# Other random offsets in the order of work: sliding-window attention with an MLP-mixer on one Trainium2 core

## The chip, the cores and the metric

The kernel runs on one core of one Trainium2 chip. The metric is the device time of one execution in microseconds (us). Lower is better. The core has five engines that run side by side: TensorE (PE, matrix products), VectorE (DVE), ScalarE (ACT), GpSimd (POOL) and SyncE (SP). In this kernel the last two do hardly more than issue transfers.

## What is computed

The inputs are q, k and v of 8 batches x 8 heads x 576 positions x 64. The attention is causal with a window of 128 positions and a linear penalty for distance (ALiBi). A mixer of two stages follows: one product pair along the positions, one along the channels, each with its residual.

```python
scores = scale * np.matmul(q, k.transpose(0, 1, 3, 2))
bias = slopes[:, None, None] * (-np.abs(rel))[None, :, :]
mask = (rel >= 0) & (rel < 128)
scores = np.where(mask, scores + bias[None], -1e9)
attn = softmax(scores)                              # per head
x = np.matmul(attn, v) -> (8, 576, 512)             # heads side by side
h = np.maximum(x.T @ w_tok1, 0.0) @ w_tok2          # 576 -> 256 -> 576
u = x + h.T
h2 = np.maximum(u @ w_ch1, 0.0) @ w_ch2             # 512 -> 1536 -> 512
return u + h2
```

## The kernel before

**Tiles.** The 576 positions of a batch are four blocks of 128 and a rest of 64. The rests of two batches share one block, the tail. Matmul operands are bf16, sums are in PSUM (eight banks, the tiles named `ps`).

**Attention of a block.** q and k are turned so that the 64 channels of a head lie on the partitions. In the first blocks PE does it (L632, and L638 copies the result to `qkT`); later SP issues a transposing DMA (L621). PE multiplies the scores (L672), ACT takes the exponential (L695, into `pe`), DVE multiplies with the mask (L705), PE multiplies with the values and a column of ones (L739), and DVE takes the reciprocal of the sum (L752) and scales (L755, into `xb`; ACT can do that in its place, L761).

**Token mixing of a batch.** The first product is L784, with L794 for the tail's rows (`xt`, copied in L779). ACT (L802) or DVE (L803) applies the relu. The second product is L827 (L823 for the tail). DVE adds the residual (L845, into `ub`). For the two opening batches the result is turned by PE (L862, copied by L868), and there L830 adds the residual on PE and ACT copies (L842). From batch 2 on SP issues transposing DMAs (L853): four of `uT` per batch, and in every second batch one of the tail, `uTt`.

**Channel mixing of a batch.** The first product is twelve chunks of four matmuls of 128x512 (L1024; in the very first batch L1009 for two of them), each followed by a relu on ACT (L1030) or DVE (L1031). For the last batch the first product goes in another form, by sums of halves (L910) and products L946, evicted in L961 to L990. The tail's first product is L1067, its relu L1072. The second product is seven smaller ones by sums of halves, which DVE makes (L1049 of the hidden values, L570 and L588 of the weights): L1212, evicted with the residual added by DVE in L1180 and stored from L1192. The tail's own is L1112 and L1119, stored from L1129. The last batch ends with L1241, L1245 and L1248.

**Where the order comes from.** Nothing of this is issued where it is written. Every operation is entered in a list with its engine, a cost, its inputs and a rank, which says when it is due (class `Plan`, L66 to 314). `run` (L118 to 299) plays the engines forward with the written costs: an engine takes, of the operations that could start first, the one of the lowest rank. Some operations have a second engine (`other`) and go to the one that would be done earlier. POOL keeps the fixed order of `LOADS` (L364) and of the later loads; SP's order follows from the ranks. `emit` (L301) writes the instructions out in planned order; on the chip each engine then runs its own list in that order and waits for what it needs. `emit` also fills planned gaps of PE up to plan time 60 us with dummy matmuls on a tile of zeros (`spin`, L1292 and L1296).

**Rounds and offsets.** `side` makes a batch's attention and token mixing, `main` its channel mixing. The opening is `side(0)`; then a round for each batch b holds `main(b)` and `side(b + 1)` (L1269 to 1283), so the next batch's attention is woven into this batch's products. The opening is part 0, the round of batch b is part b + 1. Each part has a seed:

```python
        dice = [random.Random(x) for x in SEEDS]
        for o in ops:
            if SEEDS[o.part]:
                o.rank += dice[o.part].uniform(-SHIFT, SHIFT)
```

The rank of every operation of the part is moved by a random amount of up to 1500 either way (`SHIFT`; ranks count in ns of PE's work). A seed of 0 leaves the ranks of its part alone. Ranks of the opening lie a million lower than all others.

**At the end** (L1285 to 1290), two operations on ACT of nine tiny copies each and two on DVE of five tiny memsets each are entered with a rank behind all others and may start at 262 and 266.5 us of plan time. They write to the tile of zeros and are read by nothing; ACT issues the last store (L1248) after them.

Of the kernel before, what the change touches and what calls it, by code (L numbers as in the profile page):

```python
# [10 lines left out]
ACT = mybir.ActivationFunctionType  # L11
# [54 lines left out]
class Plan:  # L66
# [6 lines left out]
    def buf(self, name, choice=None):  # L73
        return Buf(self.rings[name], choice or self.rings[name].each)
# [43 lines left out]
    def run(self):  # L118
        ops = self.ops
# [4 lines that stand above are left out]
# [210 lines left out]
RANKH = 0  # L334
RELU = 350
SUMS_AT = 60e3
SEEDS = [45795, 495947, 190309, 331881, 0, 67117, 67408, 179769, 445757]
SHIFT = 1500.0
UNIT_LATE = False
SECOND_LATE = True  # L340
# [28 lines left out]
def kernel(  # L369
# [76 lines left out]
    zero = const.tile([P, P], BF16, name="zero")  # L446
# [25 lines left out]
    pe_, act_, dve_ = nc.tensor, nc.scalar, nc.vector  # L472
# [53 lines left out]
    for i_, name in enumerate("qk"):  # L526
# [3 lines left out]
            out=buf()[:, i, :, :], in_=raw.rearrange("p (h d) -> p h d", h=H)), -100 + i_, makes=buf, after=4.8e3 + 600 * i_)  # L530
# [64 lines left out]
    for e in range(2):  # L595
        def go(e=e):
            for i in range(2):
                dve_.tensor_copy(out=maskt[:, e, :, 0, i * R : (i + 1) * R], in_=masks[:, e, :, 0, 0:R])
            dve_.tensor_copy(out=maskt[:, e, :, 1, :], in_=masks[:, e, :, 1, :])
            dve_.memset(maskt[0:R, e, :, 1, R:P], 0.0)  # L600
# [682 lines left out]
        base += n  # L1283

    for eng, n, cost, at, go in (  # L1285
            ("ACT", 9, 200, 262e3, lambda: act_.copy(out=zero[:, 0:1], in_=zero[:, 2:3])),
            ("ACT", 9, 200, 262e3, lambda: act_.copy(out=zero[:, 0:1], in_=zero[:, 2:3])),
            ("DVE", 5, 60, 266.5e3, lambda: dve_.memset(zero[:, 1:2], 0.0)),
            ("DVE", 5, 60, 266.5e3, lambda: dve_.memset(zero[:, 1:2], 0.0))):
        plan.op(eng, n * cost, lambda n=n, go=go: [go() for _ in range(n)], 1e9, after=at)  # L1290
# [41 lines left out]
```

## Time and profile before

| | before |
|---|---|
| time, median of 3 runs | 278.81 us (278.72 to 279.33) |
| time of the profiled execution | 278.47 us |
| span in its trace | 276.7 us |
| of the span: PE, DVE, ACT, POOL busy | 97%, 76%, 50%, 42% |
| PE clock granted | 1.00 |
| channel products L1024 on PE | 77.4 us in 306 recorded matmuls |
| masks L705 of 128x1024 on DVE | 30.8 us in 46, 683 ns each |
| transposing DMAs L853, issue to landing | 2.3 / 3.5 / 6.3 us (least, median, most) |

The page counts busy time for each engine. The chain is the work that ended last, followed back from the last instruction; what stands there on PE is time that only less work on PE can save, and what stands there on another engine or a transfer is time in which PE had to wait or was not yet started. "ps<-uT,WC" means that PSUM was written from the tiles `uT` and `WC`. In a timeline row the columns are the start, the length, engine and line, the operation, and how many instructions are put together in the row; square brackets hold the idle time before it and what ended it. SPq is SP issuing a transfer.

### The profile page before, as it was taken

To read this page: it belongs to the slowest core of one execution; us is meant where nothing else is said; L and a number is where in the kernel's file an instruction comes from. 1 tells how busy PE (TensorE), PEld (TensorE's weight loads), DVE (VectorE), ACT (ScalarE), POOL (GpSimd) and SP (SyncE) were. 2 spreads that over 40 slices of the span, in tenths; PEclk is the share of its full clock that TensorE was granted. 3 is DMA by queue.
4 is the path that set the end of the run, shared out by engine and by line. 5 is a ranking of instruction groups with operands and counts; after the bars stand their busy time and mean duration, and the time that the engine had idled before them with its cause. 6 is when DMAs were issued, how large, how long until landed. Compare 5 with 4: busy or idle time off the path is not lost.

```text
span 276.7 us, 6959 instructions
## 1 busy us (share of the span) xinstructions
PE 268.5 (97%) x2789; PEld 179.6 (65%) x2825; DVE 209.0 (76%) x496; ACT 139.2 (50%) x237; POOL 115.8 (42%) x146
## 2 busy tenths in 40 slices
PE   7999999999999999999999999999999999999994
PEld 3665655775686555585567655576667645679884
DVE  7577689978897469853989478763989549886984
ACT  5572884436950298107951096206860079205660
POOL 8998965940356037900585009600472220013000
PEclk9999999999999999999999999999999999999999
DMA  9999999999899999999999979999499750043014
GB/s 132 159 141 164 182 192 189 155 124 207 138 110 111 181 243 133 124 142 181 173 136 151 206 193 100 138 144 243 65 117 97 194 147 2 2 114 135 1 50 143
DMA packets 167553, 38.45 MB, mean 139 GB/s; under 512 B 155808, under 2 KB 166688, under 8 KB 167520
## 3 DMA queue, kind: packets, MB, share of 16 engines
q0 software_dynamic: 116112, 20.03, 94.9%
q1 hardware_dynamic: 50224, 17.57, 33.6%
q10 hardware_dynamic: 1184, 0.39, 0.6%
q8 instruction: 22, 0.36, 0.6%
q14 instruction: 11, 0.09, 0.1%
HBM read 35.85 MB, written 9.44 MB: 164 GB/s over the span
## 4 chain that ended last, share of the span: by engine, by line
PE 89%; DMA 4%; DVE 2%; POOL 1%; ACT 1%; issue 1%; POOLq 0%; ACTq 0%
PE ps L1212 26%; PE ps L1024 22%; PE ps L739 6%; PE ps L672 6%; PE ps L784 5%; PE ps L827 5%; PE ps L1067 4%; PE ps L1112 4%; PE ps L946 3%; DMA WC<-in_moe_w_ch_dram 3%; PE ps L1296 2%; DMA qk<-in_q_dram 2%; PE ps L632 1%; PE ps L794 1%; POOL qk L515 1%
## 5 line engine op out<-in xcount | busy, mean ns | idle before, releaser
L1024 PE MATMUL ps<-uT,WC 128*128 128x512 bf16 x306 | 77.4, 379 | 1.3 <-DMA WC<-in_moe_w_ch_dram 0.3
L695 ACT ACTIVATE pe<-ps 128x1024 bf16<-128x1024 f32 (+1 forms) x76 | 63.4, 888 | 29.9 <-PE ps L672 29.6
L515 POOL DMA_DIRECT2D v<-in_v_dram x40 | 34.1, 866 | 93.6 <-PE ps L739 88.5
L1030 ACT ACTIVATE r<-ps 128x512 bf16<-128x512 f32 x75 | 44.4, 601 | 41.1 <-PE ps L1024 39.1
L1024 PEld LDWEIGHTS <-WC 128*128 128x128 bf16 x328 | 29.1, 98 | 30.6 <-issue 1.4
L705 DVE TENSOR_TENSOR pe<-pe,mask 128x1024 bf16<-128x1024 bf16 (+1 forms) x64 | 38.2, 609 | 8.8 <-ACT pe L695 8.3
L1212 PEld LDWEIGHTS <-r 128*128 128x128 bf16 x372 | 35.9, 98 | 7.2 <-issue 0.2
L515 POOL DMA_DIRECT2D qk<-in_k_dram x39 | 34.5, 891 | 3.0 <-DMA v<-in_v_dram 1.7
L515 POOL DMA_DIRECT2D qk<-in_q_dram x39 | 34.0, 878 | 0.7 <-DMA WC<-in_moe_w_ch_dram 0.6
L1212 PEld LDWEIGHTS <-s 128*128 128x128 bf16 x288 | 27.5, 98 | 6.0 <-issue 1.3
L755 DVE TENSOR_TENSOR xb<-ps,rt 128x256 bf16<-128x256 f32 (+1 forms) x72 | 29.1, 417 | 0.7
L739 PEld LDWEIGHTS <-pe 128*128 128x128 bf16 (+1 forms) x560 | 22.3, 98 | 9.0 <-DVE pe L705 2.6
L739 PE MATMUL ps<-v,pe 128*128 128x65 bf16 (+1 forms) x560 | 26.3, 194 | 0.4 <-DVE pe L705 0.2
L1212 PE MATMUL ps<-WC,r 128*128 128x256 bf16 x192 | 25.4, 273 | 0.0
L1212 PE MATMUL ps<-WT,s 128*128 128x256 bf16 x192 | 24.6, 273 | 0.1
L845 DVE TENSOR_TENSOR ub<-ps,xb 128x512 bf16<-128x512 f32 x34 | 21.2, 683 | 1.8 <-PE ps L827 1.8
L1212 PE MATMUL ps<-WT,r 128*128 128x256 bf16 x180 | 22.4, 273 | 0.0
L672 PEld LDWEIGHTS <-qkT 64*128 64x128 bf16 x560 | 14.8, 94 | 11.2 <-issue 9.8
L1180 DVE TENSOR_TENSOR ob<-ps,ub 128x512 f32<-128x512 f32 x21 | 14.3, 686 | 9.4 <-PE ps L1212 9.2
L672 PE MATMUL ps<-qkT 64*128 64x128 bf16 (+1 forms) x304 | 19.4, 216 | 0.4
L1072 ACT ACTIVATE r2t<-ps 128x512 bf16<-128x512 f32 x12 | 7.2, 603 | 22.7 <-PE ps L1067 22.7
L752 DVE RECIPROCAL rt<-ps 128x4 f32<-128x4 f32 (+1 forms) x76 | 12.5, 175 | 7.6 <-PE ps L739 7.0
(102 smaller groups left out, 347.8 us busy)
## 6 DMA issues: line engine op xcount, KB each, us to landing
v<-in_v_dram POOLq DMA_DIRECT2D x32, 128.0 KB, 5.0
out_dram<-ob SPq DMA_DIRECT2D x16, 256.0 KB, 2.6
qk<-in_k_dram POOLq DMA_DIRECT2D x31, 128.0 KB, 5.1
qk<-in_q_dram POOLq DMA_DIRECT2D x31, 128.0 KB, 5.0
WC<-in_moe_w_ch_dram POOLq DMA_DIRECT2D x8, 384.0 KB, 8.8
out_dram<-raw SPq DMA_DIRECT2D x7, 256.0 KB, 2.7
out_dram<-ob POOLq DMA_DIRECT2D x5, 256.0 KB, 3.6
out_dram<-raw POOLq DMA_DIRECT2D x3, 256.0 KB, 2.9
```

Source lines behind the costliest of these rows:

```text
L515: nc.gpsimd.dma_start(out=to()[p0 : p0 + n, :, :], in_=rows(src, b, s0, n))
L672: pe_.matmul(wide(e)[:, i, kind, a:z], lhsT=ts[kb]()[e * D : (e + 1) * D, NHP + i, :], rhs=ts[blk]()[e * D : (e + 1) * D, i, a:z], start=n ...
L695: act_.activation(out=pb()[:, e, :, lo:, c0:c1_], in_=wide(e)[:, :, lo:, c0:c1_], func=ACT.Exp, scale=scale)
L705: dve_.tensor_tensor(out=o, in0=o, in1=heads(mk, es), op=ALU.mult)
L739: pe_.matmul(view()[a:z, at, i, :], lhsT=pb()[:, e, i, kind, a:z], rhs=vb()[:, h, 0 : D + 1], start=m == 0, stop=m == len(mms) - 1, skip_g ...
L755: dve_.tensor_tensor(out=x4(), in0=view()[r0:r1_, :, :, 0:D], in1=rt()[r0:r1_, 0:n, :, :].broadcast_to([r1_ - r0, n, 4, D]), op=ALU.mult)
L784: pe_.matmul(t1[j]()[:, :], lhsT=W1[:, c, j * P : (j + 1) * P], rhs=xb()[:, blk, :], start=c == 0, stop=False)
L845: plan.op("DVE", 690, lambda blk=blk, ht=ht, hs=hs: dve_.tensor_tensor(out=ub()[:, blk, :], in0=ht()[:, hs], in1=xb()[:, blk, :], op=ALU.a ...
L1024: pe_.matmul(ct()[:, :], lhsT=WC1[:, cb, t * P : (t + 1) * P], rhs=uT()[:, cb, :], start=cb == 0, stop=cb == NCB - 1)
L1030: plan.op("ACT", 600, lambda t=t, ct=ct: act_.activation(out=r2()[:, t, :], in_=ct()[:, :], func=ACT.Relu), rk, part=(r2, t), uses=[ct], o ...
L1180: dve_.tensor_tensor(out=v, in0=both(bk), in1=src, op=ALU.add)
L1212: pe_.matmul(of(bk, c), lhsT=l(t, c), rhs=w(t), start=first, stop=g == 1 and t == HK - 1, skip_group_check=True)
```

## The change

```diff
-SEEDS = [45795, 495947, 190309, 331881, 0, 67117, 67408, 179769, 445757]
+SEEDS = [751877, 741206, 821723, 331881, 0, 148233, 244960, 0, 319733]
...
-            ("ACT", 9, 200, 262e3, lambda: act_.copy(out=zero[:, 0:1], in_=zero[:, 2:3])),
-            ("ACT", 9, 200, 262e3, lambda: act_.copy(out=zero[:, 0:1], in_=zero[:, 2:3])),
+            ("ACT", 11, 200, 262e3, lambda: act_.copy(out=zero[:, 0:1], in_=zero[:, 2:3])),
+            ("ACT", 10, 200, 262e3, lambda: act_.copy(out=zero[:, 0:1], in_=zero[:, 2:3])),
```

The seeds of the opening, of the rounds of batches 0 and 1 and of batches 4 to 7 are others; the round of batch 6 has none now. Those of batches 2 and 3 stay. Three more tiny copies stand at the end of ACT's list. No operation is added to or taken from the computation, and `LOADS` stays as it is. What differs is the order in which operations stand on PE, DVE, ACT and SP, which engine takes those that have two, and where the dummy matmuls lie.

## The prediction

> **What bounds the kernel now.** First the page: engines, then the chain of work that ended last.
>
> ```profile
> span 276.7 us, 6959 instructions
> PE 268.5 (97%) x2789; PEld 179.6 (65%) x2825; DVE 209.0 (76%) x496; ACT 139.2 (50%) x237; POOL 115.8 (42%) x146
> ...
> PE 89%; DMA 4%; DVE 2%; POOL 1%; ACT 1%; issue 1%; POOLq 0%; ACTq 0%
> ```
>
> PE is busy 97% of the span and is 89% of the chain. A new order takes no matmul away, so it can gain only where PE waits, and lose only where it adds a wait. The view of waits on PE names the largest of them (total us, times, longest):
>
> ```profile
> PE ps L1296 <- DVE zero L479: 1.0, 1, 1.0
> ...
> PE ps L1024 <- DMA WC<-in_moe_w_ch_dram: 0.3, 1, 0.3
> ...
> PE ps L739 <- DVE pe L705: 0.2, 1, 0.2
> ```
>
> The first is the start, before any seed matters. The rest are tenths. How much the touched stretches hold in all, the view by windows tells: in each row the second number is the window's length, then PE's busy time.
>
> ```profile
> 20.00:30.00 10.00, 9.89 (x111) 6.06 (x113) 6.09 (x16) 4.85 (x10) 8.95 (x11) 1.00 1.93 169
> 30.00:40.00 10.00, 9.47 (x133) 6.05 (x132) 8.52 (x28) 8.43 (x14) 7.41 (x11) 1.00 1.78 184
> 40.00:60.00 20.00, 19.48 (x195) 13.37 (x197) 18.37 (x41) 9.30 (x15) 13.66 (x18) 1.00 2.01 169
> 60.00:80.00 20.00, 19.79 (x238) 12.96 (x240) 18.04 (x48) 14.53 (x22) 6.13 (x7) 1.00 1.46 154
> ...
> 160.00:180.00 20.00, 19.75 (x192) 11.04 (x194) 15.70 (x38) 11.79 (x17) 11.49 (x14) 1.00 1.55 140
> 180.00:200.00 20.00, 19.84 (x214) 13.93 (x216) 13.00 (x29) 10.80 (x17) 2.81 (x4) 1.00 0.88 153
> 200.00:220.00 20.00, 19.84 (x214) 14.25 (x212) 15.63 (x34) 5.86 (x8) 8.62 (x11) 1.00 1.29 128
> 220.00:240.00 20.00, 19.69 (x194) 10.85 (x197) 15.31 (x37) 13.06 (x23) 1.82 (x3) 1.00 0.27 66
> 240.00:260.00 20.00, 20.00 (x200) 16.91 (x198) 15.47 (x29) 7.78 (x15) 2.87 (x4) 1.00 0.29 87
> ```
>
> A quiet window (180 to 220) shows 0.16 us idle in 20. Above that are idle: 0.03 in 20 to 30, 0.45 in 30 to 40, 0.36 in 40 to 60, 0.05 in 60 to 80, 0.09 in 160 to 180, 0.15 in 220 to 240, nothing elsewhere. That is 1.13 us, 0.4% of the time: **the most that this change can gain**. The loss has no such bound.
>
> **The change part by part.** Built, the changed kernel has 2824 matmuls for 2825. The multiset of real matmuls, and the number of switches between their shapes, are the same. PE's list is the same up to 20.2 us, in nine blocks from 34.6 to 44.8 us, and from 90.1 to 161.0 us (batches 2 and 3), and again in the last products. POOL's list is the same. So PE's own work changes by one dummy matmul only: 592 columns in two become 408 in one, 184 less. At 0.65 / 1536 us a column (three matmuls of 512 columns from 44.80 to 45.45, rows below) that is -0.08 us.
>
> **Opening, up to 36 us.** The chain and PE's timeline:
>
> ```profile
> 25.92 0.89 POOL v L515
> ...
> 28.52 7.42 DMA WC<-in_moe_w_ch_dram
> ```
>
> ```profile
> 35.99 1.04 PE L1024 MATMUL ps<-uT,WC 128*128 128x512 bf16 x4 [0.32 <-DMA WC<-in_moe_w_ch_dram]
> ...
> 41.18 0.66 PE L739 MATMUL ps<-v,pe 128*128 128x65 bf16 x16 [0.24 <-DVE pe L705]
> ...
> 44.54 0.42 PE L739 MATMUL ps<-v,pe 128*128 128x65 bf16 x8
> 44.80 0.81 PE L784 MATMUL ps<-xb,W 128*128 128x512 bf16 x3
> 45.45 0.41 PE L739 MATMUL ps<-v,pe 128*128 128x65 bf16 x8
> ```
>
> PE arrives at the fifth kind of chunk 0.32 us before the weights' load (issued 28.52, landing 35.94). The load keeps its place on POOL, three loads behind the one of 25.92. The chain has L862 ahead of that one, but L862 does not read the `v` tile that it fills; the products that do (L739) end before 20.2 us in either order, and what it waits for is an earlier load. So nothing that moves sets the load's time. Whatever the new order saves before 36 us, the 0.08 included, ends in this wait: **0**. It costs something only if PE comes over 0.32 us later than now.
>
> **36 to 45 us.** PE's blocks are the same; on DVE one weight sum (L570) changes places with one sum of hidden values (L1049), both about 0.55 us. The waits at 41.18 and 44.54 stay: 0. At 44.80 the old order has three L784 (0.65) between two groups of values; the new one has one (0.22). The second group needs the second of these masks:
>
> ```profile
> 43.80 1.28 DVE L705 TENSOR_TENSOR pe<-pe,mask 128x1024 bf16<-128x1024 bf16 x2
> ```
>
> It ends at 45.08, and the 44.50 to 44.54 step that the chain shows as "issue" takes 0.05 after a mask. The new order reaches the values at 44.80 + 0.22 = 45.02 and waits until 45.13: **+0.11**. From either side: 0 (DVE earlier by its last operation's overlap) to +0.2.
>
> **45 to 90 us.** DVE is busy 18.37 and 18.04 of 20 us here, so this is where orders differ. Some alternatives change engines:
>
> ```profile
> L755 DVE TENSOR_TENSOR xb<-ps,rt 128x256 bf16<-128x256 f32 (+1 forms) x72 | 29.1, 417 | 0.7
> ...
> L845 DVE TENSOR_TENSOR ub<-ps,xb 128x512 bf16<-128x512 f32 x34 | 21.2, 683 | 1.8 <-PE ps L827 1.8
> ```
>
> DVE gets one copy L638 and one relu L803 more (each one operation of 512 or 1024 columns, about 0.68 by the nearest row), one L755 more (0.42), and gives three L868 (0.42 each, as many columns out of PSUM as an L755 costs) and one L1031 (0.68) to ACT: 1.78 less 1.94, nothing. Following each product back to its DVE and ACT inputs, with the durations of this execution, I find places with 30 to 70 ns to spare and none plainly late. I take **+0.1**, between 0 and one displaced operation (0.4).
>
> **94 us.** The four turned blocks of batch 2 are issued with one store among them, but their sums come earlier: 0 to +0.2, taken as **+0.05**.
>
> **Batch 5, 174 to 190 us.** PE, SP and DVE, and the line of the transposes (least, median, most):
>
> ```profile
> 174.63 1.89 PE L827 MATMUL ps<-r,W 128*128 128x512 bf16 x8
> 176.45 0.62 PE L823 MATMUL ps<-r,W2t 128*64 128x512 bf16 x4
> 177.01 1.04 PE L1024 MATMUL ps<-uT,WC 128*128 128x512 bf16 x4
> ...
> 183.78 1.47 PE L1212 MATMUL ps<-WT,r 128*128 128x256 bf16 x12
> 185.09 1.89 PE L1024 MATMUL ps<-uT,WC 128*128 128x512 bf16 x7
> ...
> 190.28 1.07 PE L1067 MATMUL ps<-uTt,WC 128*128 128x128 bf16 x16
> ```
>
> ```profile
> 175.98 2.52 SPq L853 DMA_TRANSPOSE uT<-ub  x2
> 178.60 1.22 SPq L853 DMA_TRANSPOSE uTt<-ub  x1
> 179.87 3.54 SPq L853 DMA_TRANSPOSE uT<-ub  x2
> ```
>
> ```profile
> L853 SPq DMA_TRANSPOSE uT<-ub x24: 1190/1232/2225, 87.2 to 247.8; - x24
> ...
> DMA to landing us min/median/max: 2.3/3.5/6.3
> ```
>
> Between L827, whose sums are turned, and L1024, which uses them, lie 10.46 us. The new order moves the four L1024 of 177.01 (0.87) and twelve L1212 (12 of 0.109, 1.31) ahead of L827, and sixteen L1067 (1.07 less the 0.16 by which a row is longer than its steps, 0.91) in between. So L827 starts at 176.81, L1024 can start at 186.00, and 9.19 us are left. The first transpose then is issued at 176.81 + 1.35 = 178.16, and the fifth four steps later: of 1.29 each (175.98 to 179.87 is three), at 183.32. In the old order the last was issued at 179.87 + 3.54 - 1.26 = 182.15, and L1024 came at 185.09, straight after twelve steps of L1212: so it took at most 2.9, and by the row at least 2.3. Then it lands between 185.6 and 186.2: 0 to +0.2, and I take **0**. `uTt`, third in line, is now needed at 185.09: issued at 180.74, it lands at 184.2 by the median.
>
> The row of landings runs from 2.3 to 6.3. The Trainium skill, "DMA: Bandwidth & Descriptors", section "Issuing engines are not separate DMA queues", says that transfers started by SP and POOL run on the same 16 DMA engines and interleave. By that rule the transposes share with POOL's loads wherever they are issued, and at 6.3 the last would land at 189.6, for +3.6; the bound of 2.9 above speaks against that for the last of them.
>
> **Batch 6, 220 us.**
>
> ```profile
> 220.45 0.59 PE L1112 MATMUL ps<-WC,r2t 128*128 128x512 bf16 x2
> 221.03 1.02 PE L1024 MATMUL ps<-uT,WC 128*128 128x512 bf16 x4
> ```
>
> Two steps of 0.217 end at 220.88; 0.15 is a wait for the turned blocks. The new order leaves some 2.6 us more between their sums and this L1024, so it goes: **-0.15**. The 0.09 over the quiet level in 160 to 180 I count by half, **-0.05**.
>
> **The end.**
>
> ```profile
> 264.18 2.00 ACT L1286 COPY zero<-zero 128x1 bf16<-128x1 bf16 x9
> ...
> 273.64 0.36 ACTq L1248 DMA_DIRECT2D out_dram<-ob  x1
> ```
>
> Three more copies of 0.22 us end near 268.9; ACT's store waits for DVE until 273.64. Cover 4.7 us: **0**. The last batch's products are mixed anew; window 240 to 260 shows no idle time, and I find no input late: 0.
>
> **Sum**: 0 + 0.11 + 0.1 + 0.05 + 0 - 0.15 - 0.05 = +0.06 us on the profiled execution's 278.47 (span 276.7 and 1.77 outside it, unchanged). That execution lies 0.34 under the median of 278.81, so the forecast is **278.9 us**.
>
> **Rivals.** (1) *Slower: the turned blocks of batch 5 come late.* One of the five issues took 2.2 us instead of 1.23 (the row's most; it is in the 3.54). If it does again, the last is issued at 184.3 and lands at 186.6 to 187.2, a wait of 0.6 to 1.2 where none was: about 279.7. It decides as soon as issue and landing together pass 186.0 - 178.16 = 7.8 us; they would take 7.5 to 8.1 without the long issue. For it: the distance shrinks by 1.27 us; against: the long issue is one of 24. (2) *Slower: DVE becomes late in 45 to 90 us.* Two inputs, each late by one operation of 0.42 that is now ahead of it, less 0.07 to spare, give +0.7: about 279.6. It decides where more than 0.07 us of DVE's work is put ahead of an input that PE takes next. For it: DVE's 90%; against: its total does not grow. (3) *Faster: the waits go.* If the new order clears the excess of 40 to 60 (0.36), 160 to 180 and 220 to 240 (0.24), it gives -0.6 on 278.81: 278.2. Against: the two mask waits stand in blocks that do not change. (4) *Faster: the weights' load was not the limit.* If it lands earlier, as DVE leaves POOL other times to issue, up to 0.32: 278.3 with the 0.15 of batch 6. (5) *The change does nothing*, the orders being equal: excluded, they differ in four stretches.
>
> **How the numbers follow.** Forecast 0.47; (1) 0.18; (2) 0.14; (3) 0.17; (4) 0.04. About 0.2%, 0.56 us, is what a measurement of this kernel tells from no change. Faster: (3), 0.17; within: the forecast and (4), 0.51; slower: (1) and (2), 0.32. The range runs from (3) to just above (1): 278.2 to 279.8; beyond lie the 1.13 bound below and a late `uTt` above. The likeliest case alone: 278.5 to 279.3.
>
> **What would show it.** In the changed kernel's trace: L1024 still waiting for the load that lands near 35.9; a new wait of about 0.1 at the values near 45.0; windows 40 to 60 and 60 to 80 within 0.2 of 19.48 and 19.79; L1024 after sixteen L1067 near 186.0 with no idle time before it (a transpose named there makes (1) right); no wait near 221. The prediction is wrong if a new wait of over 0.5 us stands anywhere, or if the load near 36 us lands at another time.

## The result, and the profile after

The changed kernel takes **281.84 us** (median of 6 runs, 281.26 to 282.92), the kernel before **279.19 us** beside it (6 runs, 278.72 to 280.33). The ratio is 1.0096, with an interval of 1.0072 to 1.0119: **2.65 us slower**, between 2.0 and 3.3. The prediction, 278.9 in a range of 278.2 to 279.8, was wrong. The profiled execution took 281.66 us.

The page of the profile after: span, busy time by engine, and the chain of work that ended last.

```profile
span 279.9 us, 6968 instructions
PE 268.7 (96%) x2790; PEld 179.8 (64%) x2824; DVE 210.7 (75%) x496; ACT 138.7 (50%) x237; POOL 115.8 (41%) x146
...
PE 72%; DVE 8%; POOL 7%; DMA 5%; issue 3%; SPq 2%; ACT 1%; DVEq 0%; ACTq 0%; POOLq 0%
```

PE is busy 268.7 us for 268.5, so its own work is as forecast; the span grew by 3.2 us of waiting. PE's share of the chain fell from 89% to 72%. Outside the span lie 1.76 us for 1.77. The view of waits on PE, after:

```profile
PE ps L632 <- DMA qk<-in_q_dram: 1.5, 2, 1.1
...
PE ps L1212 <- DVE raw L1180: 0.7, 1, 0.7
PE ps L1024 <- DMA uT<-ub: 0.3, 1, 0.3
```

The first two were not in the forecast, and for the third it had 0.05. The windows, after (length, then PE's busy time):

```profile
20.00:30.00 10.00, 8.76 (x102) 5.39 (x99) 5.79 (x15) 3.92 (x9) 8.07 (x11) 1.00 1.84 160
30.00:40.00 10.00, 9.50 (x134) 6.19 (x135) 8.24 (x26) 7.41 (x13) 8.17 (x10) 1.00 1.79 184
40.00:60.00 20.00, 19.41 (x176) 12.30 (x179) 19.71 (x44) 10.35 (x16) 13.70 (x17) 1.00 1.93 160
60.00:80.00 20.00, 19.75 (x250) 13.19 (x251) 16.82 (x45) 13.82 (x23) 5.03 (x6) 1.00 1.37 148
80.00:100.00 20.00, 19.35 (x172) 13.16 (x174) 13.53 (x28) 5.68 (x13) 6.36 (x8) 1.00 1.55 155
...
220.00:240.00 20.00, 19.75 (x193) 10.92 (x195) 13.46 (x34) 12.45 (x19) 2.52 (x4) 1.00 0.32 80
240.00:260.00 20.00, 19.35 (x185) 16.16 (x184) 16.66 (x32) 5.50 (x10) 2.88 (x4) 1.00 0.37 87
```

The row of before for 80 to 100:

```profile
80.00:100.00 20.00, 19.84 (x179) 12.65 (x181) 13.05 (x28) 6.02 (x15) 5.25 (x6) 1.00 1.40 154
```

Against the rows of before PE lost 1.13 us in 20 to 30, 0.49 in 80 to 100 and 0.65 in 240 to 260. From 40 to 80 and from 220 to 240 it is within 0.07.

To add the losses up I take PE's **lateness**: the time at which a matmul starts, less the time that all PE work ahead of it takes when each step lasts what it usually lasts in the trace of before. A wait raises it by its whole length (at 251 us by 0.82, of which the view of waits shows 0.65, since it counts from the end of the matmul before). Between the two profiled executions it grows as follows.

| place | lateness gained against before | what is there |
|---|---|---|
| up to 46.8 us | +1.26 | loads; a mask |
| 96 us | +0.37 | turned blocks of batch 2 |
| 122 and 221 us | -0.34 | two waits of before that are gone |
| 251 us | +0.82 | an eviction L1180 |
| 274 us | +0.10 | an eviction L1180 |
| last product to the end of the span | +1.01 | the last store |
| sum | 3.22 | of 3.2 |

**Up to 46.8 us.** PE, after:

```profile
27.96 0.62 PE L632 MATMUL ps<-ident,qk 128*128 128x128 bf16 x8 [1.12 <-DMA qk<-in_q_dram]
...
30.52 0.62 PE L632 MATMUL ps<-ident,qk 128*128 128x128 bf16 x8 [0.37 <-DMA qk<-in_q_dram]
...
36.24 1.89 PE L1024 MATMUL ps<-uT,WC 128*128 128x512 bf16 x7
```

PE waits for two loads of q, and not for the weights' load that the prediction watched. Yet that load still decides. In this execution it was issued at 29.21 and landed at 36.87. The first four L1024 of 36.24 use older weights. The fourth starts at 36.89, and PE begins to read the new weights at 36.91, which is 0.04 after they landed, as it is in all 18 profiles of this study. So PE could not have gone on earlier: without the waits for q it would have waited here. The next rows are a mask, as forecast:

```profile
45.84 0.38 PE L784 MATMUL ps<-xb,W 128*128 128x512 bf16 x1
46.19 0.42 PE L739 MATMUL ps<-v,pe 128*128 128x65 bf16 x8
```

One L784 takes 0.22, and the values come at 46.19 instead of 46.06, waiting for a mask: 0.13.

**96 us and 187 us**, the turned blocks of batches 2 and 5:

```profile
96.03 1.89 PE L1024 MATMUL ps<-uT,WC 128*128 128x512 bf16 x8 [0.30 <-DMA uT<-ub]
```

```profile
186.43 1.06 PE L1067 MATMUL ps<-uTt,WC 128*128 128x128 bf16 x16
187.54 1.04 PE L1024 MATMUL ps<-uT,WC 128*128 128x512 bf16 x3
```

At 187.54 there is no wait. The last of the four blocks landed at 187.50.

**251 us.** PE, then DVE, after:

```profile
251.42 1.47 PE L1212 MATMUL ps<-WT,r 128*128 128x256 bf16 x12 [0.65 <-DVE raw L1180]
```

```profile
248.61 0.76 DVE L910 TENSOR_TENSOR tt<-uT 128x512 bf16<-128x512 bf16 x2 [0.93 <-DMA uT<-ub]
249.29 0.68 DVE L1180 TENSOR_TENSOR ob<-ps,ob 128x512 f32<-128x512 f32 x1
249.89 0.88 DVE L910 TENSOR_TENSOR tt<-uT,tt 128x512 bf16<-128x512 bf16 x2
250.68 0.68 DVE L1180 TENSOR_TENSOR raw<-ps,raw 128x512 f32<-128x512 f32 x1
```

And DVE before:

```profile
250.43 0.69 DVE L1180 TENSOR_TENSOR ob<-ps,ub 128x512 f32<-128x512 f32 x1 [1.51 <-PE ps L1212]
251.04 0.75 DVE L910 TENSOR_TENSOR tt<-uT 128x512 bf16<-128x512 bf16 x2
```

Before, the halves L910 stand behind the evictions. After, they stand ahead of them, and the first waits 0.93 for the turned block until 248.61. The eviction behind it, whose product is ready, waits with it. PE needs the PSUM tile that the second eviction empties.

**The end.** The source view of the last stores (L1248), before and after, from issue to landing:

```profile
DMA to landing us min/median/max: 1.8/1.9/2.1
```

```profile
DMA to landing us min/median/max: 2.5/2.8/3.1
```

The two stores are the same 128 KB each. ACT issues the last one 0.77 us after PE's last product starts, in both kernels (275.83 after). In the DMA view after, from 277.5 to 278 us, stands

```profile
q14 instruction: 1, 0.01, 3.9%
```

one packet of 8 KB of instructions, at 277.61. The store is issued at 275.83, 15 of the 16 parts of its completion are in by 277.94, and the sixteenth comes at 278.96. Before, the same fetch runs at 272.66, ahead of the issue at 273.64.

The Trainium skill, "Runtime: NRT & Kernel Launch", section "Instruction fetch mechanics", says that a sequencer fetches its next page of code through a DMA queue of its own and that the cost is mostly hidden. The trace has instruction packets on queues apart from the data, q14 and q8, which agrees. Behind the issue of the last store the cost is not hidden: it is 1.0 us.

### The profile page after: what moved, and what is told of

Read it like the earlier page. It is cut to its first block, busy times and chain, and to the rows that moved or that the text cites. A ratio compares the mean times of both kernels' runs of the same rounds, so it can differ in the third digit from the quotient of the medians.

```text
span 279.9 us, 6968 instructions
## 1 busy us (share of the span) xinstructions
PE 268.7 (96%) x2790; PEld 179.8 (64%) x2824; DVE 210.7 (75%) x496; ACT 138.7 (50%) x237; POOL 115.8 (41%) x146
## 4 chain that ended last, share of the span: by engine, by line
PE 72%; DVE 8%; POOL 7%; DMA 5%; issue 3%; SPq 2%; ACT 1%; DVEq 0%; ACTq 0%; POOLq 0%
PE ps L1024 23%; PE ps L1212 19%; PE ps L739 6%; PE ps L672 5%; POOL qk L515 4%; PE ps L784 4%; PE ps L1067 4%; PE ps L946 3%; PE ps L1112 3%; DMA qk<-in_q_dram 3%; DMA uT<-ub 3%; PE ps L827 3%; DVE ub L845 2%; POOL v L515 2%; SPq L853 2%
## 5 line engine op out<-in xcount | busy, mean ns | idle before, releaser
L1024 PE MATMUL ps<-uT,WC 128*128 128x512 bf16 x306 | 77.7, 379 | 1.4 <-DMA uT<-ub 0.3
L1024 PEld LDWEIGHTS <-WC 128*128 128x128 bf16 x328 | 28.9, 97 | 29.0 <-issue 1.0
L1212 PEld LDWEIGHTS <-r 128*128 128x128 bf16 x372 | 35.7, 98 | 8.1 <-issue 1.9
L1212 PEld LDWEIGHTS <-s 128*128 128x128 bf16 x288 | 27.8, 98 | 6.0 <-issue 1.1
L755 DVE TENSOR_TENSOR xb<-ps,rt 128x256 bf16<-128x256 f32 (+1 forms) x73 | 29.3, 416 | 0.7
L1212 PE MATMUL ps<-WC,r 128*128 128x256 bf16 x192 | 25.6, 273 | 0.0
L1212 PE MATMUL ps<-WT,s 128*128 128x256 bf16 x192 | 24.3, 273 | 0.0
L1212 PE MATMUL ps<-WT,r 128*128 128x256 bf16 x180 | 22.1, 273 | 0.7 <-DVE raw L1180 0.7
L845 DVE TENSOR_TENSOR ub<-ps,xb 128x512 bf16<-128x512 f32 x34 | 21.1, 682 | 0.7 <-PE ps L827 0.7
L1180 DVE TENSOR_TENSOR ob<-ps,ub 128x512 f32<-128x512 f32 x20 | 13.7, 686 | 9.8 <-PE ps L1212 9.8
```

Of the source, the lines that this page charges most:

```text
L755: dve_.tensor_tensor(out=x4(), in0=view()[r0:r1_, :, :, 0:D], in1=rt()[r0:r1_, 0:n, :, :].broadcast_to([r1_ - r0, n, 4, D]), op=ALU.mult)
L845: plan.op("DVE", 690, lambda blk=blk, ht=ht, hs=hs: dve_.tensor_tensor(out=ub()[:, blk, :], in0=ht()[:, hs], in1=xb()[:, blk, :], op=ALU.a ...
L1024: pe_.matmul(ct()[:, :], lhsT=WC1[:, cb, t * P : (t + 1) * P], rhs=uT()[:, cb, :], start=cb == 0, stop=cb == NCB - 1)
L1180: dve_.tensor_tensor(out=v, in0=both(bk), in1=src, op=ALU.add)
L1212: pe_.matmul(of(bk, c), lhsT=l(t, c), rhs=w(t), start=first, stop=g == 1 and t == HK - 1, skip_group_check=True)
```

## The experiments

There are two theories, and the trace of after speaks for each in part. The loss comes from the **places** of the new order that let a wait through: the opening, batch 2, the last batch. Or it comes from the **tail**, the time from the start of PE's last product to the end of the span: the last store lands late, through the extra copies or through the order. And there are two for the opening: the new **order** brings the loads later, or the **load** lands at a time that changes from one execution to the next, and the first profile of before was an early one.

### One part of the change at a time

e1: the old order with the new copies. e2: the new order with the old copies. e3: the new offsets of the first three parts alone, e4: of the last four alone, both with the old remainder.

```diff
 # e1, against before
-            ("ACT", 9, 200, 262e3, ...
-            ("ACT", 9, 200, 262e3, ...
+            ("ACT", 11, 200, 262e3, ...
+            ("ACT", 10, 200, 262e3, ...
 # e2, against before
-SEEDS = [45795, 495947, 190309, 331881, 0, 67117, 67408, 179769, 445757]
+SEEDS = [751877, 741206, 821723, 331881, 0, 148233, 244960, 0, 319733]
 # e3, against before
-SEEDS = [45795, 495947, 190309, 331881, 0, 67117, 67408, 179769, 445757]
+SEEDS = [751877, 741206, 821723, 331881, 0, 67117, 67408, 179769, 445757]
 # e4, against before
-SEEDS = [45795, 495947, 190309, 331881, 0, 67117, 67408, 179769, 445757]
+SEEDS = [45795, 495947, 190309, 331881, 0, 148233, 244960, 0, 319733]
```

> The old seeds with 11 and 10 copies at the end of ACT's list; PE's list is that of the kernel before. Theory 'code load by the copies': the three copies move the place where an engine fetches its next 8 KB of code, and the fetch falls on the last store as in the changed kernel (last store's landing 1.0 us later than before): +1.0 us, ratio 1.0035, and the trace has an 8 KB fetch about 2 us after the last store's issue. Rival 'order': the late landing comes from the new order of the last batch, and the copies cost nothing: ratio 1.000, the fetch stays about 1 us ahead of the last store's issue.

> The new seeds with 9 and 9 copies; PE's list is that of the changed kernel. Theory 'code load by the copies': the end is as before, 1.0 us off the changed kernel's 281.8, so about 280.8, ratio 1.006. Rival 'order': ratio 1.0096 as the changed kernel has. Theory 'loads' for the opening: PE waits about 1.1 us near 28 us for a q load and 0.4 near 30.5 again; rival 'luck of one execution': these waits are another size, or gone, with the same order.

> New seeds for the opening and the rounds of batches 0 and 1, old ones for the rest, 9 and 9 copies. Theory 'the opening's order costs': the +1.1 us at 28 us, +0.1 at 46 and +0.3 at 96, less 0.2 at 122, are there: ratio 1.0045 to 1.005. Rival 'luck of one execution': the loads land as in the kernel before, and only +0.2 to +0.4 is left: ratio 1.001.

> Old seeds for the opening and the rounds of batches 0 to 3, new ones for batches 4 to 7, 9 and 9 copies. Theory 'the last rounds cost': the wait of 0.65 us for an eviction (L1180) near 250 us is there and the one of 0.15 near 221 is not: +0.5, ratio 1.002; with the late landing of the last store on top, if that comes from the order, ratio 1.0055. Rival 'all of it is the opening': ratio 1.000.

| kernel | us | ratio to before (278.57) | last product to end of span |
|---|---|---|---|
| e1 copies | 279.07 | 1.0016 (1.0003 to 1.0028) | 3.80 |
| e2 offsets | 281.20 | 1.0097 (1.0075 to 1.0118) | 4.76 |
| e3 opening | 279.71 | 1.0034 (1.0017 to 1.0051) | 3.80 |
| e4 late rounds | 280.74 | 1.0096 (1.0070 to 1.0123) | 4.81 |

The last column is 3.80 in before and 4.81 in after. The copies don't make the tail; the late rounds do. They carry the larger loss, and the opening about 1 us. The sum of e3 and e4, 1.3%, is more than e2's 0.97%, within their intervals. In e4's own profile I find only 1.3 to 1.5 us of its 2.7: that execution (280.22) was the lowest of its six.

e4 also shows the wait of batch 5 that after missed by 0.04 us:

```profile
186.61 1.04 PE L1024 MATMUL ps<-uT,WC 128*128 128x512 bf16 x3 [0.27 <-DMA uT<-ub]
```

Of the eight profiles with the new late rounds four have such a wait, of 0.24 to 0.47, and four none. No profile with the old ones has it.

### The last batch and the tail

e5 is after, with each of the halves L910 put behind an eviction L1180, as before had them. e6 is after, with three groups of five tiny memsets more on DVE, ahead of three earlier evictions: that moves the place of the code at which DVE stands. Both work on the list that `emit` sorts.

```diff
-        for _, _, go in sorted(work, key=lambda w: w[:2]):
+        for _, _, go in sorted(moved(self, work), key=lambda w: w[:2]):
...
 # e5: h are the halves, e the evictions from the first half on, put gives an operation another place
+    put.update({o: (e[i // 2].t0, e[i // 2].n + 0.1 * (1 + i % 2)) for i, o in enumerate(h)})
 # e6: five are the five memsets, ev all evictions
+    work = work + [(ev[k].t0, ev[k].n - 0.1, five.emit) for k in [30, 34, 41]]
```

> The changed kernel, its planned order kept on every engine but for one spot on DVE: the four sums of halves (L910) of the last batch stand behind the two evictions (L1180) that they stood ahead of. Theory 'head of the queue': in the changed kernel the first L910 waited on DVE for a turned block, with the evictions that PE needs behind it, and PE lost 0.65 us near 251; now that wait is gone, 0.5 to 0.65 us off, ratio to the kernel before about 1.0075. Rival 'the eviction itself is late' (its product or its buffer): the wait stays, ratio 1.0096.

> The changed kernel with fifteen tiny memsets more on DVE, five each ahead of three evictions (L1180) for which DVE has 0.9, 2.6 and 1.9 us idle; all else in the same order. Theory 'code load': the 8 KB fetch near 266 us comes when DVE has run a fixed number of instructions (543 to 545 of those recorded, in every run so far) and the one near 277.6 some 11.2 us after it; fifteen instructions earlier it falls before the last store, which then lands 2.1 us after its issue and not 3.1: -1.0 us, ratio about 1.006. Rival 'the stores themselves': the late landing comes from the two stores issued close together in the new order, the end stays 4.6 us after PE's last product, ratio 1.0096.

e5: 281.05 us for 278.89, 1.0090 (1.0064 to 1.0116). Its DVE and PE:

```profile
247.41 0.69 DVE L1180 TENSOR_TENSOR ob<-ps,ob 128x512 f32<-128x512 f32 x1 [0.50 <-PE ps L1212]
248.02 0.75 DVE L910 TENSOR_TENSOR tt<-uT 128x512 bf16<-128x512 bf16 x2
248.72 0.69 DVE L1180 TENSOR_TENSOR raw<-ps,raw 128x512 f32<-128x512 f32 x1
```

```profile
249.40 0.60 PE L946 MATMUL ps<-uT,WC 128*128 128x256 bf16 x4
249.84 1.36 PE L1212 MATMUL ps<-WT,r 128*128 128x256 bf16 x11
```

The eviction now waits for its product, and PE goes from L946 to L1212 in 0.44, four steps of 0.109, without idle time. So the place of the halves made that wait: shown in the trace, where the wait is gone in e9 and e12 too, which have the same edit. In the time the gain is smaller than the interval.

e6: 280.11 us, 1.0058 (1.0035 to 1.0080), 1.1 us less than after by the ratios, whose intervals overlap by a little. The fetch ran at 273.02, ahead of the last store (276.44), which landed like this:

```profile
DMA to landing us min/median/max: 2.2/2.2/2.2
```

The tail is 3.82 us again. So the fetch that runs behind the last store's issue makes the late landing. I had reckoned that it would come 11.2 us behind the fetch before it, as in after (266.44 and 277.61); it came 5.7 behind.

What sets its place shows in the number of DVE's records of every kind, the issuing ones included: in all the profiles of this study the last fetch runs when DVE has done 574 to 577 of them. The old order has 582 in all (581 recorded in one profile), the new late rounds 578, and e6, e9 and e12 592. With 578 only three are left, and the last store is out; with 582 five are left, ahead of the last evictions. DVE's operations are 496 in both orders; the four records that the new late rounds lack are waits for semaphores (79 in after for 83 in before). Every profile of a kernel with 578 (after, e2, e4, e5, e8) has a tail of 4.75 to 4.92 us, every other one that I measured 3.80 to 3.85.

### The opening

e7 is the kernel before, with one of POOL's loads of v moved from ahead of the weights' load to behind it. e10 is before, with the masks of 41.2 and 44.5 us ahead of what DVE had in front of them.

```diff
 # e7
+    pool = sorted((o for o in plan.ops if o.eng == "POOL"), key=lambda o: o.order)
+    put[pool[26]] = (pool[32].t0, pool[32].n + 0.1)
 # e10
+    dve = sorted((o for o in plan.ops if o.eng == "DVE"), key=lambda o: (o.t0, o.n))
+    put[dve[63]] = (dve[62].t0, dve[62].n - 0.1)
+    put[dve[69]] = (dve[73].t0, dve[73].n + 0.1)
```

> The kernel before, planned order kept on every engine, but on POOL one load of v (the one whose values PE multiplies at 36.9 us) is issued behind the weights' load that PE waits for at 36 us, so that this and five other loads are issued one place earlier. Theory 'the loads set the opening': PE's wait there goes and the waits for q near 27 to 28 us shrink: -0.3 to -0.85 us, ratio 0.997 to 0.999. Rival 'PE or DVE sets it': the load lands earlier and PE comes no earlier, or v is late in its place: ratio 1.000 or above.

> The kernel before, all in its order but two places on DVE: the mask that PE waits for at 41.2 us stands ahead of a scaling (L755, 0.43 us), and the two masks of 43.8 us ahead of a weight sum (L570, 0.53 us). Theory 'DVE's order sets these waits': the waits of 0.27 and 0.29 us at 41.2 and 44.5 go and nothing takes their place: -0.4 to -0.55 us, ratio 0.998. Rival 'the next input is late': the scaling or the weight sum is late in its place, or the exponential is: ratio 1.000.

e7: 278.48 us for 278.89, 0.9994 (0.9975 to 1.0012). The chain:

```profile
27.47 8.82 DMA WC<-in_moe_w_ch_dram
```

Issued 1.05 us earlier than in before, the load landed 0.36 later, after 8.82 us instead of 7.42. As the landing differs by 1.3 us between profiles of the old order (table below), one profile can't tell what a place in POOL's list is worth for it; the time shows no gain above 0.7 us. The Trainium skill, "DMA: Bandwidth & Descriptors", section "Issuing engines are not separate DMA queues", says that transfers interleave on 16 shared engines. A landing that does not follow its issue would fit that, but no run here shows the interleaving.

e10: 278.81 us for 278.83, 1.0002 (0.9985 to 1.0019). Two waits of 0.31 and 0.29 fell to 0.18 and 0.07, and waits of 0.10 to 0.17 came at 43.9, 48.1 and 52.6 us, where DVE's scalings L755 and L845 are now later. The masks are not to be had for nothing: what DVE does later in their place makes PE wait in turn.

e11 is e1 a second time, e13 and e15 the kernel before, e14 and e16 e3's kernel, one profile each, for the landing of the load.

> A second profile of the old order (with the three copies more, as in the first run on them). Theory 'luck of one execution': PE waits between 0 and 1.1 us for a q load near 27 us, another size than the 1.1 that this kernel's first profile had. Rival 'the order or the copies set it': 1.1 us again.

> The kernel before, a second profile. In all profiles so far PE passes 46 us a fixed time after the landing of the weights' load near 36 us (31.8 us of its own work behind it in the new order, 32.1 in the old). Theory 'luck': that landing lies anywhere from 35.9 to 37.8 in either order. Rival 'the order moves it': with the old order 35.9 to 36.9, as in six profiles.

> The new opening with the old rest, a second profile. Theory 'luck': the landing lies anywhere from 35.9 to 37.8. Rival 'the order moves it': 36.5 to 37.8, as in seven profiles of the new opening.

> The kernel before, a third profile. Theory 'luck': the landing of the weights' load anywhere from 35.9 to 37.8. Rival 'the order moves it': 35.9 to 36.9.

> The new opening with the old rest, a third profile. Theory 'luck': the landing anywhere from 35.9 to 37.8. Rival 'the order moves it': 36.5 to 37.8.

They took 278.76 (e11), 278.95 (e13), 279.04 (e14), 279.55 (e15) and 279.91 us (e16), with before at 278.83 beside e11 and at 278.67 beside the others. e1 and e11 are one program; their waits for q:

```profile
PE ps L632 <- DMA qk<-in_q_dram: 0.9, 1, 0.9
```

```profile
PE ps L632 <- DMA qk<-in_q_dram: 0.4, 2, 0.2
```

So the wait for q changes from one execution to the next, in the old order too. The landing of the weights' load over all 18 profiles, and PE's lateness at 46.8 us:

| opening | landing, us | landing less lateness |
|---|---|---|
| old, 9 profiles | 35.94 (before) to 37.19, mean 36.47 | 32.07 to 32.15, e10 32.39 |
| new, 9 profiles | 35.69 to 37.84, mean 36.93, after 36.87 | 31.80 to 31.97 |

Two things stand in this table. First, whatever waits come ahead of it, PE goes on from the landing: the last column is the same within 0.17 us in every kernel of a row but e10, where two masks are earlier. Second, at one and the same landing the new order is 0.3 us later; 0.13 of that is the mask at 46.19, the rest lies in smaller steps. The landing itself varies by 1.3 and 2.2 us. Before's first profile was the earliest of its nine; e14, in the new order, was earlier still. The means differ by 0.46, with standard errors of 0.13 and 0.23: whether the order moves the landing at all **stays open**.

### Batch 2, and what is left

e8 is after, with the store between the transposes of batch 2 moved behind them. e9 is after with three things undone: the halves behind, the memsets, and the second L632 of the opening back behind twelve L1009. e12 is e4 with the halves and the memsets.

```diff
 # e8
+    sp = sorted((o for o in plan.ops if o.eng == "SP"), key=lambda o: (o.t0, o.n))
+    put[sp[11]] = (sp[13].t0, sp[13].n + 0.1)
 # e9: e5's and e6's lines, and
+    late = pe[49].t0
+    for i, o in enumerate([pe[49]] + [o for o in plan.ops if o.eng == "DVE" and pe[49].bufs[0] in o.bufs]):
+        put[o] = (pe[52].t0, pe[52].n + 0.1 * (i + 1))
 # e12: e5's and e6's lines, on e4
```

> The changed kernel with one store (L1192) moved on SP's queue from between the four transposing DMAs of batch 2 to behind them; all else the same. Theory 'the store holds SP': the last two blocks land 0.6 us earlier and the wait of 0.3 to 0.57 us near 96 us goes: -0.3 to -0.5 us, ratio about 1.008. Rival 'the blocks' sums are late': the wait stays, 1.0096.

> The changed kernel with three places put back and all else in its order: the sums of halves behind the two evictions (as in the run before on that), the fifteen tiny memsets that bring the code fetch forward, and on PE one block of turns (L632) behind the twelve L1009 that it had been put ahead of, with its copy. Theory 'these three places': 0.65, 1.0 and some 0.5 us off, ratio to the kernel before 1.001 to 1.003, where +0.1 at 46 us, the wait at 96 us and that of 0 to 0.4 at 187 us are left. Rival 'the order costs elsewhere too': ratio 1.005 or above.

> The old opening with the new order of the last four rounds, and in it the sums of halves behind the two evictions and the fifteen tiny memsets. Theory 'these two places are the late rounds' cost': what is left is 0 to 0.4 us at 187 us and 0.1 at the last product, less 0.15 at 221: ratio 1.000 to 1.002. Rival 'the late order costs elsewhere too', as the ratio of 1.0096 of the late rounds alone was above the 1.0055 that the places in its profile add up to: ratio 1.004 or above.

e8: 280.99 us for 278.89, 1.0102 (1.0071 to 1.0133), no gain. SP and PE:

```profile
88.74 6.18 SPq L853 DMA_TRANSPOSE uT<-ub  x4
95.02 0.53 SPq L1192 DMA_DIRECT2D out_dram<-ob  x1
```

```profile
97.04 1.24 PE L1024 MATMUL ps<-uT,WC 128*128 128x512 bf16 x5 [0.46 <-DMA uT<-ub]
```

Without the store the four issues take 6.18 us. With it, after's first to last take 6.54 (87.89 to 94.43), of which 0.6 is the store; before's four take 5.51:

```profile
87.89 2.55 SPq L853 DMA_TRANSPOSE uT<-ub  x2
90.53 0.54 SPq L1192 DMA_DIRECT2D out_dram<-ob  x1
91.13 3.30 SPq L853 DMA_TRANSPOSE uT<-ub  x2
```

```profile
87.18 5.51 SPq L853 DMA_TRANSPOSE uT<-ub  x4
```

From the first issue to the time at which PE could have used the blocks lie 7.84 us in after and in e8 (96.03 less 0.30 less 87.89; 97.04 less 0.46 less 88.74), and 7.32 in before. So the new order does give the blocks 0.5 us more, but SP takes longer over them: from the first to the last 6.1 to 7.4 us in the nine profiles with the new opening, and 5.3 to 5.8 in eight of the nine with the old. In the ninth, e15, it took 6.85. A pair at the usual 1.2 to 1.3 a piece takes 2.5; in after's second pair one issue takes about 2, and in e8, where nothing stands between the four, 1.1 us are lost as well. The wait is in eight of nine profiles with the new opening, 0.30 to 1.15 us, and in two of nine with the old (e13, e15). The largest, from e16, and that of e15:

```profile
96.28 1.02 PE L1024 MATMUL ps<-uT,WC 128*128 128x512 bf16 x4 [1.15 <-DMA uT<-ub]
```

```profile
95.90 1.89 PE L1024 MATMUL ps<-uT,WC 128*128 128x512 bf16 x8 [0.74 <-DMA uT<-ub]
```

The means are 0.51 and 0.13, so this place costs about 0.4 us. The store can only be a part of it: with the store gone from there, e8 keeps wait and time.

What stands beside a long issue, the traces tell. Each profile has 22 packets of 16 KB of instructions on q8, of 0.9 to 2.0 us each. In the DMA view after, from 91 to 91.3 us, stands

```profile
q8 instruction: 1, 0.02, 20.1%
```

This packet starts at 91.07 and takes 0.97; the issue of about 2 us starts at 91.13. Of the 486 issues L853 in the 18 profiles, the 393 that overlap no packet of q8 take 1.19 to 1.34 us, and all the 68 that take longer (1.39 to 2.95) overlap one. In e6 the packet, at 91.29, met the store, which took 0.54 in after:

```profile
91.23 2.08 SPq L1192 DMA_DIRECT2D out_dram<-ob  x1
```

So a long issue goes with a fetch of instructions. That the fetch causes it was not tried by a run. In all 18 profiles one of these packets overlaps an issue of batch 2, in either order, so this alone does not say why the new order loses more there: that **stays open**.

e9: 279.80 us for 278.83, 1.0043 (1.0021 to 1.0066). e12: 279.36 for 278.69, 1.0019 (1.0002 to 1.0037). With the halves and the fetch put right, the late rounds lose 0.2% instead of 1.0%: these two places are most of their loss. In e9 the L632 that was put back no longer waits, but the first waits 1.1 and the landing (36.94) still decides; what is left of e9's 0.4% is the opening and batch 2.

No version beats the kernel before.

## Why the prediction was wrong

Both signs of being wrong that the prediction named came in the trace of after: new waits of over 0.5 us (1.12 at 28 us, 0.65 at 251 us), and the load near 36 us landing at another time (36.87).

**PE's own work**: right. 268.7 us for 268.5, with one dummy less.

**Opening, "Whatever the new order saves before 36 us ... ends in this wait: 0".** The mechanism is right: in all 18 profiles PE goes on from the load, though in four of them (after, e5, e8, e14) it came only 0.02 to 0.04 us too early for it. What failed is its size: the step took the landing of one execution, 35.94, for the landing. It lies between 35.7 and 37.8, and the base of the sum was the earliest of nine. To that come 0.2 us of small steps from 36 to 46 us that were put at 0.

**44.8 us, +0.11**: right, 0.13.

**45 to 90 us, +0.1**: right within what can be seen; the windows 40 to 60 and 60 to 80 are 0.07 and 0.04 lower.

**94 us, +0.05**: mis-sized. It measured about +0.4. The sums do come earlier (7.84 us to use them in for 7.32), but SP takes 0.6 to 1.8 us longer from the first issue to the last. The most of the row of issues, 2225 ns, was set against batch 5 as a rival and not against batch 2. Three of before's 24 issues were long (1.59, 1.60 and 2.23 us), each beside a fetch of instructions.

**Batch 5, 0, and rival (1)**: a hairline, as forecast. 0 in four profiles and 0.24 to 0.47 in four; mean 0.17. Rival (1) happens in half of these profiles, at less than half of its price.

**Batch 6, -0.15**: the wait is gone, as forecast. But it is gone in profiles with the old order of these rounds too, where PE comes later (e1, e7, e11, e15): it belonged to the early first profile, and to the median it counts hardly anything. The 0.19 at 122 us is of the same kind.

**"The last batch's products are mixed anew ... I find no input late: 0."** This step failed. The input that is late is not an operand but a PSUM tile, freed by an eviction that stands on DVE behind a half waiting for a transfer. By the view PE waits 0.65, 0.47, 0.15 and 0.66 in after, e2, e4 and e8, which is 0.82, 0.63, 0.32 and 0.82 of lateness, and hardly at all (0.06) in e6, all with the halves ahead: 0.5 of lateness on the mean.

**The end, "Cover 4.7 us: 0" and the tail taken as it was.** The copies cost nothing, as forecast (e1's tail is 3.80). The tail grew by 1.0 all the same. The prediction set ACT's three copies against 4.7 us of cover, and counted the operations that change engines. It did not count DVE's waits for semaphores, four fewer, by which the fetch falls behind the last store's issue. This step failed too, and no rival had it.

The sum by places, against a median: 0.3 (opening) + 0.4 (96 us) + 0.2 (187) + 0.5 (251) + 1.0 (tail) + 0.1 (274) = 2.5 us, and up to 0.5 if the new opening does bring the load later. Measured: 2.65, between 2.0 and 3.3. So both theories hold for a part, and the tail is the largest single one.

## What to carry to other kernels

A wait that absorbs a gain is worth no more than its transfer's landing is steady: profile the same program some times before taking a landing as given. Where an order is changed, follow the blocks that stand ahead of an eviction on an in-order engine, not only PE's operands. And look at where the fetches of instructions fall, behind the last store's issue above all: one packet there cost 1.0 us here, and its place followed the number of all of DVE's instructions, waits included.

## What the runs showed that I had not expected

- A fetch of 8 KB of instructions between the last store's issue and its landing delays one of its 16 parts by 1.02 us (277.94 to 278.96) and with it the end. Fifteen tiny memsets on DVE moved it away and gave 1.0 us back in the tail (4.81 to 3.82).
- Loads issued at the same place of the same list land at times that differ by over a microsecond between executions (35.94 to 36.55 in three profiles of the kernel before and 36.46 to 36.93 in two of e1; 35.69 to 36.70 in three of e3's).
- A transposing issue by SP (L853) that usually takes 1.2 to 1.3 us takes 1.4 to 2.95 in 68 of 486 cases, each of them beside a 16 KB packet of instructions on q8, and four in a row without anything between them took anywhere from 5.3 to 6.85 us in the old order.
